# Retention and expert routing on one core: the last tiles' indirect transfers and the q, k, v loads tied to TensorE

## The chip, the cores and the metric

The kernel runs on one core of a Trainium2 chip. The engines of that core are TensorE (PE; its weight loads are listed as PEld), VectorE (DVE), ScalarE (ACT), GpSimd (POOL) and SyncE (SP), and 16 DMA engines move data. The metric is device microseconds of one execution; the comparison is of medians of several runs.

## The reference

Two parts follow each other. The first is an attention without softmax and with a decay per head; its output is cut into rows x of 512 numbers, one for each of the 4608 tokens. The second sends every token to the one expert of eight that has the largest logit.

```
ret = (q @ k.T / 8) * where(i >= j, gamma[h] ** (i - j), 0)       # 8 x 8 heads, 576 positions, 64 wide
x = (ret @ v) as rows [4608, 512]
logits = x @ w_gate;  e = argmax(logits);  p = softmax(logits)[e]
eom = sigmoid(x @ w_output_gate)[e]
out[token] = p * eom * (relu(x[token] @ w1[e]) @ w2[e])            # w1 512 x 1024, w2 1024 x 512
```

## The kernel before

The first phase goes through 36 tiles of 128 tokens (`for g in range(NTILE)`; nine tiles are two batches). The order on each engine is the order in which the code is written (`manual_schedule`). For a tile g TensorE computes the scores (`scores`, one tile ahead), the state's part and the tile's own part of the output (`out_x`), the update of the state (`update`) and the transposed k rows of the next tile (`k_rows`). GpSimd scales q (`prep_q`) and v (`prep_v`) by the decay, two tiles ahead and from tile 7 on three. ScalarE copies the output from PSUM (`xT`), VectorE turns it into rows (`x_rows`), and SyncE stores these to memory (`store_x`, tensor `xs`). The tensor `pack` holds q, k and v of a tile side by side; `load` fetches all of it, 768 KB, in one transfer into one of seven buffers `pk`, six tiles ahead from tile 8 on.

Every four tiles make a gate group: logits on TensorE, `gate_a` on VectorE (it begins with a transposition of the logits and ends with the choice `oh` and its count `cum`), `ranks` on TensorE, `gate_b`, `gate_d`, `gate_c`. The group then has four scatters, one for each tile, in the list `todo`: each writes a token's number, weight and row into `lst`, the list of its expert (`scatter`, an indirect DMA that GpSimd issues). Once the list's first rows are complete, `load_idx` reads them and `gather` fetches tokens' rows from `xs` by further indirect DMAs of GpSimd, into tiles `w2h`, `w2l` and later `x_q`. How many scatters and gathers go out in a tile is a table, `puts` and `mine`; nothing else holds GpSimd back from issuing them:

```
puts = {16: 2, 17: 2, 18: 0, 19: 0, 24: 2, 25: 2, 27: 2, 28: 2, 30: 0, 31: 0, 35: 5}.get(g, 1)
mine = {23: 1, 24: 1, 25: 1, 26: 1, 28: 1, 29: 2, 30: 1, 31: 1, 32: 1, 33: 2}.get(g, 0)
```

Behind the tiles the second phase begins: `mm1` is a strip of 12 products of the first expert matrix, and its argument `at` names products at which one entry of `todo` is issued. The first strip stands between the last logits and the last `ranks`. From here on gathers are tied to TensorE one at a time: `tc.add_manual_dep(i.ins, last[0].name, SYNC, ...)` makes GpSimd wait until the product `last[0]` is done. SyncE's transfers are issued in the order of the code; each waits until the eighth before it has landed.

Of the kernel before, what the change touches and what calls it, by code (L numbers as in the profile page):

```python
# [10 lines left out]
F32 = mybir.dt.float32  # L11
# [10 lines left out]
B, H, S, D = 8, 8, 576, 64  # L22
# [4 lines left out]
P = 128  # L27
NP = H // 2
# [23 lines left out]
def tile_retention_moe(  # L52
# [126 lines left out]
        xps.append(a[:, 1].rearrange("p (k n) -> p k n", k=KB))  # L179
    pools = {"xt0": xta, "ht0": hpa}  # L180

    last = [None]

    def gather(e, t, u, paced=False):
        if u == 0 and e == 0 and t < TA:
            make_gidx(0, t, t + 1, G)
        if u == 0 and (e, t) not in XG:
            XG[e, t] = pools["xq"].tile([P, 4, P], F32, name="x_q")
        seen = xs if e or t >= TA else xs[0:4 * P * (READY[t] + 1) * GT]
        i = G.indirect_dma_start(out=XG[e, t][:, u, :], out_offset=None, in_=seen,  # L190
                                 in_offset=bass.IndirectOffsetOnAxis(ap=gidx[:, e, 4 * t + u:4 * t + u + 1], axis=0))
        if paced:
            tc.add_manual_dep(i.ins, last[0].name, SYNC, reason="one gather to a stretch of products")

    def size(e, part):
        return N1[e] if part else R0[e]
# [171 lines left out]
    pk, qs, vs, kn, xT, xr, gt = {}, {}, {}, {}, {}, {}, {}  # L368
    st_ps, stcur = [None], [None]

    def load(g):
        pk[g] = ld.tile([P, 3, 512], F32, name="pk")
        SP.dma_start(out=pk[g], in_=pack[g])

    def load_first():
        for g in range(5):
            pk[g] = ld.tile([P, 3, 512], F32, name="pk")
        A.dma_start(out=pk[0][:, 0], in_=pack[0, :, 0])
        SP.dma_start(out=gq_sb[:, :, 0:P], in_=gq)
        SP.dma_start(out=pk[0][:, 1], in_=pack[0, :, 1])  # L380
        A.dma_start(out=cmat_sb[:, 0], in_=cmat[:, 0])
        SP.dma_start(out=ident, in_=ident_d)
        A.dma_start(out=pk[0][:, 2], in_=pack[0, :, 2])
        SP.dma_start(out=gkf, in_=gk)
        SP.dma_start(out=pk[1], in_=pack[1])
        SP.dma_start(out=wg_sb, in_=wg)
        SP.dma_start(out=pk[2], in_=pack[2])
        SP.dma_start(out=pk[3], in_=pack[3])
        SP.dma_start(out=pk[4], in_=pack[4])

    def more_gq(c):
        w = P if c < 4 else 64
# [6 lines left out]
    def prep_q(g):  # L399
        c = g % CPB  # L400
        c0 = P * c if c < 5 else 64 + P * (c - 5)
        qs[g] = pk[g][:, 0].rearrange("p (n i) -> p n i", n=NP)
        (V if g < 2 else G).tensor_tensor(out=qs[g], in0=qs[g], in1=gq_sb[:, :, c0:c0 + P], op=ALU.mult)

    def prep_v(g):
        v = vs[g] = pk[g][:, 2].rearrange("p (h d) -> p h d", d=D)
        n = 5 if g > 22 else 0
        for h in range(n):
            A.activation(out=v[:, h], in_=v[:, h], func=AF.Copy, scale=gk_sb[:, g % CPB, h])
        G.tensor_tensor(out=v[:, n:H], in0=v[:, n:H], in1=gk_sb[:, g % CPB, n:H].broadcast_to([P, H - n, D]),  # L410
                        op=ALU.mult)

    def k_rows(g):

        kt = ps_1.tile([P, 512], F32, name="kt")
        for p in range(NP):
            T.transpose(kt[:, P * p:P * p + P], pk[g][:, 1, P * p:P * p + P], ident)
        kn[g] = wk.tile([P, 512], F32, name="kn")
        if g % CPB == 4:
            for i in range(2):  # L420
                v = [a.rearrange("t (a b c) -> t a b c", a=2, b=2)[:, :, i] for a in (kn[g], kt)]
                A.activation(out=v[0], in_=v[1], func=AF.Copy, scale=half[:, i:i + 1])
        else:
            A.copy(out=kn[g], in_=kt)

    def scores(g):


        sc = [banks[(2 * g + r) % 3] for r in range(2)]
        S_sb = wk.tile([P, 2, NP, P], F32, name="S_sb")  # L430
        edge = g % CPB == 4
        for pp in (0, 2):
            for late in range(2):
                for p in (pp, pp + 1):
                    h = (late + p) % 2
                    i = slice(64, P) if late else slice(0, 64) if edge else slice(0, P)
                    for r in range(2):
                        s = slice(64 * r, 64 * r + 64)
                        T.matmul(sc[r][64 * h:64 * h + 64, p, i], lhsT=pk[g][s, 1, P * p + 64 * h:P * p + 64 * h + 64],  # L439
                                 rhs=qs[g][s, p, i], start=True, stop=True, skip_group_check=True)  # L440
        m = cmat_sb[:, 1 if edge else 0].rearrange("p (a b) i -> p a b i", a=1).broadcast_to([P, 2, 2, P])
        for r in range(2):
            V.tensor_tensor(out=S_sb[:, r].rearrange("p (a b) i -> p a b i", a=2),  # L443
                            in0=sc[r].rearrange("p (a b) i -> p a b i", a=2), in1=m, op=ALU.mult)
        return S_sb

    def update(g):
        c = g % CPB
        if c == 8:
            return  # L450
        if c in (0, 4):
            st_ps[0] = ps_1.tile([P, NP, D], F32, name="st_ps")
        for p in range(NP):
            for r in range(2):
                o = P * p + 64 * r
                T.matmul(st_ps[0][64 * r:64 * r + 64, p, :], lhsT=kn[g][:, o:o + D], rhs=vs[g][:, 2 * p + r, :],
                         start=(c in (0, 4) and p == 0), stop=True, skip_group_check=True)
        A.copy(out=stT[g % 2], in_=st_ps[0])
        stcur[0] = stT[g % 2]

    def out_x(g, S_sb, state):
        c = g % CPB
        o = o_ps[:, :, 256 * (g % 2):256 * (g % 2) + 256]
        part = lambda p, r: o[64 * ((p + r) % 2):64 * ((p + r) % 2) + 64, r, P * (p // 2):P * (p // 2) + P]
        order = [(p, (p + i) % 2) for p in range(NP) for i in range(2)]
        if state is not None:
            w = 64 if c == 4 else P
            for p, r in order:
                s = slice(64 * r, 64 * r + 64)
                T.matmul(part(p, r)[:, 0:w], lhsT=state[s, p, :], rhs=qs[g][s, p, 0:w],  # L470
                         start=(p < 2), stop=False, skip_group_check=True)
        for p, r in order:
            T.matmul(part(p, r), lhsT=vs[g][:, 2 * p + r, :], rhs=S_sb[:, r, p, :],
                     start=(state is None and p < 2), stop=True, skip_group_check=True)
# [589 lines left out]
```

## Time and profile before

| | |
|---|---|
| median of three runs | 588.22 us (586.67 to 591.13) |
| the profiled execution's own time | 594.7 us |
| its span in the profile | 592.6 us |
| mean granted TensorE clock | 0.98 |
| PE busy | 558.9 us, 94% |
| PEld busy | 519.0 us, 88% |
| DVE, ACT, POOL busy | 367.0, 179.0, 329.7 us |
| DMA | 105.86 MB, mean 179 GB/s |

The profile is of one execution, which took longer than the median of the runs. The first phase reaches to about 165 us of the span. A granted clock of 1.00 is 2.4 GHz and 0.50 is 1.2 GHz. An idle time is written in square brackets with what ended it; "issue" means that the profile shows nothing that the engine waited for, "remote" that the releasing event is not one of an instruction of the trace.

### The profile page before, as it was taken

The page shows a single profiled execution, that of the slowest core. Times are in us where ns is not written, and L with a number is a line of the kernel's source. Part 1 is how long each engine was busy: PE and PEld are TensorE (multiplying, and loading weights), DVE is VectorE, ACT ScalarE, POOL GpSimd, SP SyncE. Part 2 cuts the span into 40 slices and gives each one's busy share as a digit, 9 for nine tenths or more (in the row PEclk, how much of TensorE's full clock was granted, in tenths as well). Part 3 has the DMA queues.
Part 4 walks back from the last instruction along what each step waited for, and adds up shares of the span by engine and source line. Part 5 has one row for each costly group of instructions (what it writes and reads, how often), then busy time and mean ns, then how long its engine had stood idle before and what let it go on. Part 6 is the DMA issues. An engine that isn't in the chain of part 4 may idle for free. (4 is left out here: it accounts for less than half of the span.)

```text
span 592.6 us, 14974 instructions
## 1 busy us (share of the span) xinstructions
PE 558.9 (94%) x5886; PEld 519.0 (88%) x5886; DVE 367.0 (62%) x805; ACT 179.0 (30%) x419; POOL 329.7 (56%) x359
## 2 busy tenths in 40 slices
PE   6989998999769989999999999999999999999994
PEld 4878887778569989998999899899999989999993
DVE  3668887678547465884576378457636747755440
ACT  4524435566114122420421232042123204213011
POOL 3848886889454576664555264345527526624602
PEclk9989998999879999999999999999999999999999
DMA  8989987796102475645643664464356455543123
GB/s 335 363 294 324 299 294 251 232 322 205 59 25 70 132 206 177 207 147 146 193 151 106 189 202 132 112 221 158 113 178 213 141 145 167 166 124 130 45 56 114
DMA packets 50069, 105.86 MB, mean 179 GB/s; under 512 B 10190, under 2 KB 24719, under 8 KB 49998
## 3 DMA queue, kind: packets, MB, share of 16 engines
q1 hardware_dynamic: 40254, 84.53, 44.8%
q0 software_dynamic: 9312, 19.71, 10.3%
q8 instruction: 47, 0.77, 0.5%
q10 hardware_dynamic: 432, 0.66, 0.4%
q14 instruction: 24, 0.20, 0.1%
HBM read 79.67 MB, written 25.33 MB: 177 GB/s over the span
## 5 line engine op out<-in xcount | busy, mean ns | idle before, releaser
L190 POOL DMA_INDIRECT x_q<-xs,gidx x139 | 149.4, 1075 | 90.2 <-PE y_ps L289 36.5
L242 PE MATMUL h_ps<-xh,w1h 128*128 128x256 f32 (+5 forms) x512 | 154.1, 301 | 0.4 <-DVE hl L245 0.4
L242 PE MATMUL h_ps<-xl,w1h 128*128 128x256 f32 (+5 forms) x512 | 153.9, 301 | 0.3 <-DVE xl L224 0.3
L242 PE MATMUL h_ps<-xh,w1l 128*128 128x256 f32 (+5 forms) x512 | 153.7, 300 | 0.0
L242 PEld LDWEIGHTS h_ps<-xh,w1h 128*128 128x128 f32 x512 | 97.2, 190 | 1.3 <-DVE hl L245 0.7
L242 PEld LDWEIGHTS h_ps<-xl,w1h 128*128 128x128 f32 x512 | 97.1, 190 | 0.8 <-DVE xl L224 0.5
L242 PEld LDWEIGHTS h_ps<-xh,w1l 128*128 128x128 f32 x512 | 97.9, 191 | 0.0
L244 ACT ACTIVATE hh<-h_ps 128x256 fp32r<-128x256 f32 (+5 forms) x128 | 52.4, 415 | 134.9 <-PE h_ps L242 110.0
L245 DVE SCALAR_TENSOR_TENSOR hl<-h_ps,hh 128x256 fp32r<-128x256 f32 (+5 forms) x128 | 57.8, 458 | 51.9 <-ACT hh L244 41.5
L289 PE MATMUL y_ps<-hh,w2l 128*128 128x360 f32 (+3 forms) x256 | 81.2, 317 | 0.0
L289 PE MATMUL y_ps<-hl,w2h 128*128 128x360 f32 (+3 forms) x256 | 81.2, 317 | 0.0
L289 PE MATMUL y_ps<-hh,w2h 128*128 128x360 f32 (+3 forms) x256 | 81.2, 317 | 0.0
L443 DVE TENSOR_TENSOR S_sb<-sc,cmat_sb 128x512 f32<-128x512 f32 x72 | 45.9, 679 | 22.7 <-PE sc L439 21.0
L223 ACT CAST xh<-x_t 128x512 fp32r<-128x512 f32 (+4 forms) x36 | 21.3, 592 | 122.3 <-DVE x_t L219 84.8
L224 DVE TENSOR_TENSOR xl<-x_t,xh 128x512 fp32r<-128x512 f32 (+4 forms) x36 | 23.8, 660 | 53.5 <-ACT xh L223 51.1
L248 POOL DMA_INDIRECT out_dram<-y,idx x15 | 15.3, 1018 | 67.1 <-ACT y L272 60.4
L248 POOL DMA_INDIRECT out_dram<-yr,idx x24 | 26.7, 1113 | 44.1 <-ACT yr L315 42.5
L439 PE MATMUL sc<-pk 64*64 64x64 f32 (+1 forms) x1152 | 38.4, 256 | 12.6 <-issue 7.2
L439 PEld LDWEIGHTS sc<-pk 64*64 64x64 f32 x1152 | 30.6, 139 | 21.5 <-issue 20.0
L167 DVE TENSOR_TENSOR w1l<-st,w1h 128x1024 fp32r<-128x1024 f32 (+1 forms) x36 | 47.9, 1330 | 2.1
L263 PE MATMUL y_ps<-w2h,hl 128*128 128x512 f32 x120 | 46.8, 390 | 2.0 <-DVE hl L245 2.0
L575 POOL DMA_INDIRECT lst<-ents,sli x36 | 37.0, 1029 | 20.6 <-DVE ents L571 15.0
(137 smaller groups left out, 970.1 us busy)
## 6 DMA issues: line engine op xcount, KB each, us to landing
st<-in_w_dram SPq DMA_DIRECT2D x64, 512.0 KB
pk<-in_pack_dram SPq DMA_DIRECT2D x35, 768.0 KB
xs<-xq SPq DMA_DIRECT2D x36, 256.0 KB
yr<-yg SPq DMA_DIRECT2D x16, 256.0 KB
yg<-yt SPq DMA_DIRECT2D x16, 176.0 KB
x_q<-xs,gidx POOLq DMA_INDIRECT x139
yg<-yt SPq DMA_DIRECT2D x12, 160.0 KB
yr<-yg SPq DMA_DIRECT2D x4, 208.0 KB
```

What stands on the lines that cost most here:

```text
L167: V.tensor_tensor(out=lo[:, k], in0=st[:, k], in1=hi[:, k].bitcast(F32), op=ALU.subtract)
L190: i = G.indirect_dma_start(out=XG[e, t][:, u, :], out_offset=None, in_=seen, in_offset=bass.IndirectOffsetOnAxis(ap=gidx[:, e, 4 * t + u:4 ...
L224: return lambda: V.tensor_tensor(out=lo, in0=src[:, :, 0:n], in1=hi.bitcast(F32), op=ALU.subtract)
L242: last[0] = T.matmul(ps, lhsT=a[:, k, :], rhs=b[:, k, :], start=(j == 0), stop=(j == 3 * KB - 1)).ins
L244: A.activation(out=hh, in_=ps, func=AF.Relu)
L245: V.scalar_tensor_tensor(out=hl, in0=ps, scalar=0.0, in1=hh.bitcast(F32), op0=ALU.max, op1=ALU.subtract)
L248: i = G.indirect_dma_start(out=out, out_offset=bass.IndirectOffsetOnAxis(ap=rows, axis=0), in_=y, in_offset=None, bounds_check=NT - 1, oob ...
L263: last[0] = T.matmul(ps, lhsT=a[:, c0:c0 + n], rhs=b, start=(j == 0), stop=(j == 3 * FB - 1)).ins
L289: last[0] = T.matmul(ps[:, 0:n], lhsT=a, rhs=b, start=(j == 0), stop=(j == 3 * FB - 1)).ins
L439: T.matmul(sc[r][64 * h:64 * h + 64, p, i], lhsT=pk[g][s, 1, P * p + 64 * h:P * p + 64 * h + 64], rhs=qs[g][s, p, i], start=True, stop=Tru ...
L443: V.tensor_tensor(out=S_sb[:, r].rearrange("p (a b) i -> p a b i", a=2), in0=sc[r].rearrange("p (a b) i -> p a b i", a=2), in1=m, op=ALU.mult)
L575: i = G.indirect_dma_start(out=lst, out_offset=bass.IndirectOffsetOnAxis(ap=sli[:, t, :], axis=0), in_=ent[:, t], in_offset=None)
```

## The change

Two things change. First, the scatters and gathers of the last three tiles are tied to products of TensorE, two to a tile: the two gathers of tile 33 to the last state product (mark `q`) and the last own product (mark `v`) of that tile, two scatters each of tiles 34 and 35 likewise, and two more to the first strip's products. One scatter moves forward to tile 31. The load of the list for the fourth tile of the first expert moves behind the first strip. Second, `pack` is laid out with q, k and v one behind the other, and each is loaded by a transfer of its own into a buffer of its own; from the sixth tile on they wait for the marks `q`, `v` and `u` (the last product of `update`) of the tile six before.

```diff
+    last, marks = [None], {}
+    def gather(e, t, u, paced=False, by=None):
...
-        if paced:
-            tc.add_manual_dep(i.ins, last[0].name, SYNC, reason="one gather to a stretch of products")
+        if paced or by:
+            tc.add_manual_dep(i.ins, (by or last[0]).name, SYNC, reason="one gather to a stretch of products")
...
-    def load(g):
-        pk[g] = ld.tile([P, 3, 512], F32, name="pk")
-        SP.dma_start(out=pk[g], in_=pack[g])
+    def load(g, i, by=None):
+        pk[g, i] = ld.tile([P, 512], F32, name="qkv"[i])
+        j = SP.dma_start(out=pk[g, i], in_=pack[g, i])
+        if by:
+            tc.add_manual_dep(j.ins, by.name, SYNC, reason="one transfer to a stretch of products")
...
     def update(g):
         c = g % CPB
+        marks["u"] = marks["v"]
...
+                i = T.matmul(st_ps[0][64 * r:64 * r + 64, p, :], lhsT=kn[g][:, o:o + D], rhs=vs[g][:, 2 * p + r, :],
+                             start=(c in (0, 4) and p == 0), stop=True, skip_group_check=True)
+                marks["u"] = i.ins
...
+                marks["q"] = T.matmul(part(p, r)[:, 0:w], lhsT=state[s, p, :], rhs=qs[g][s, p, 0:w],
+                                      start=(p < 2), stop=False, skip_group_check=True).ins
+        marks.setdefault("q", last[0])
...
+            marks["v"] = T.matmul(part(p, r), lhsT=vs[g][:, 2 * p + r, :], rhs=S_sb[:, r, p, :],
+                                  start=(state is None and p < 2), stop=True, skip_group_check=True).ins
...
-        def scatter(t):
+        def scatter(t, by=None):
...
+            if by:
+                tc.add_manual_dep(i.ins, (by[0] if by is last else by).name, SYNC,
+                                  reason="one scatter to a stretch of products")
...
-        for t in (g + 5,) if g < 8 else (g + 5, g + 6) if g == 8 else (g + 6,):
-            if t < NTILE:
-                load(t)
+        if g == 0:
+            for i in range(3):
+                load(5, i)
...
-        puts = {16: 2, 17: 2, 18: 0, 19: 0, 24: 2, 25: 2, 27: 2, 28: 2, 30: 0, 31: 0, 35: 5}.get(g, 1)
-        mine = {23: 1, 24: 1, 25: 1, 26: 1, 28: 1, 29: 2, 30: 1, 31: 1, 32: 1, 33: 2}.get(g, 0)
+        puts = {16: 2, 17: 2, 18: 0, 19: 0, 24: 2, 25: 2, 27: 2, 28: 2, 30: 0, 33: 0, 34: 0, 35: 0}.get(g, 1)
+        mine = {23: 1, 24: 1, 25: 1, 26: 1, 28: 1, 29: 2, 30: 1, 31: 1, 32: 1}.get(g, 0)
...
+        if g == 33:
+            gather(0, *divmod(got, 4), by=marks["q"])
+            gather(0, *divmod(got + 1, 4), by=marks["v"])
+        elif g > 33:
+            for m in "qv":
+                todo.pop(0)(by=marks[m])
         x_rows(g)
...
         update(g)
+        if g + 6 < NTILE:
+            for i, m in enumerate("qvu"):
+                load(g + 6, i, marks[m])
...
-    load_idx(0, TA, TA + 1)
     gate_a(NG - 1)
     exp_a(NG - 1)
-    mm1(0, 0, 0)
+    todo[:] = [partial(f, by=last) for f in todo]
+    mm1(0, 0, 0, (1, 7))
+    load_idx(0, TA, TA + 1)
...
-        "pack": np.ascontiguousarray(np.stack([tr(nat(q)), tr(swapped(nat(k))), swapped(nat(v))], axis=2)),
+        "pack": np.ascontiguousarray(np.stack([tr(nat(q)), tr(swapped(nat(k))), swapped(nat(v))], axis=1)),
```

The up-front loads of tiles 0 to 4 are split in the same way. What moves on GpSimd is shown from the scatter of tile 32 on; `L575` is the scatter, `L190` a gather, `L559` a small addition for the next gate, and in brackets stand the semaphores waited for (DMASW: earlier indirect transfers; PE, DVE, Pool: engines). Before:

```order
L574 MEMSET tick 128x1
L575 DMA lst<-ents,sli 37888x16 [waits DMASW2_49,DVE_49]
L190 DMA w2l_107<-xs,gidx 128x128 [waits DMASW3_49]
L190 DMA w2l_107<-xs,gidx 128x128 [waits DMASW4_49]
L574 MEMSET tick 128x1 [waits Pool_49]
L575 DMA lst<-ents,sli 37888x16 [waits DMASW5_49]
L574 MEMSET tick 128x1 [waits Pool_49]
L575 DMA lst<-ents,sli 37888x16 [waits DMASW6_49]
L559 TENSOR_TENSOR base_81<-csm_sb,bump 128x1 [waits DVE_49]
L574 MEMSET tick 128x1 [waits Pool_49]
L575 DMA lst<-ents,sli 37888x16 [waits DMASW7_49]
L574 MEMSET tick 128x1 [waits Pool_49]
```

On GpSimd from the same scatter of tile 32 on, now (the scatter is `L580`, the addition `L564`):

```order
L579 MEMSET tick 128x1 [waits Pool_49]
L580 DMA lst<-ents,sli 37888x16 [waits DMASW3_49]
L190 DMA w2l_107<-xs,gidx 128x128 [waits DMASW4_49,PE_49]
L190 DMA w2l_107<-xs,gidx 128x128 [waits DMASW5_49,PE_49]
L579 MEMSET tick 128x1 [waits Pool_49]
L580 DMA lst<-ents,sli 37888x16 [waits DMASW6_49,PE_49]
L579 MEMSET tick 128x1 [waits Pool_49]
L580 DMA lst<-ents,sli 37888x16 [waits DMASW7_49,PE_49]
L564 TENSOR_TENSOR base_81<-csm_sb,bump 128x1 [waits DVE_49]
L579 MEMSET tick 128x1 [waits Pool_49]
L580 DMA lst<-ents,sli 37888x16 [waits DMASW0_49,DVE_49,PE_49]
L579 MEMSET tick 128x1 [waits Pool_49]
```

The instructions and their order are the same; two gathers and every scatter from here to the first strip wait for TensorE as well. On SyncE, around the weights' load (`L149`) of tile 10, `L373` is a load of q, k and v and `L485` the store of a tile's rows (DMAHW: earlier transfers of SyncE). Before:

```order
L373 DMA pk<-in_pack_dram 128x1536 [waits DMAHW7_49,PE_49,Pool_49]
L485 DMA xs<-xq 128x512 [waits DMAHW0_49,DVE_49]
L149 DMA st<-in_w_dram 128x1024 [waits DMAHW1_49]
L373 DMA pk<-in_pack_dram 128x1536 [waits DMAHW2_49,PE_49,Pool_49]
L485 DMA xs<-xq 128x512 [waits DMAHW3_49,DVE_49]
L373 DMA pk<-in_pack_dram 128x1536 [waits DMAHW4_49,PE_49,Pool_49]
```

On SyncE at the same place now (the store is `L490`):

```order
L490 DMA xs<-xq 128x512 [waits DMAHW5_49,DVE_49]
L149 DMA st<-in_w_dram 128x1024 [waits DMAHW6_49]
L373 DMA q<-in_pack_dram 128x512 [waits DMAHW7_49,PE_49]
L373 DMA k<-in_pack_dram 128x512 [waits DMAHW0_49,PE_49]
L373 DMA v<-in_pack_dram 128x512 [waits DMAHW1_49,PE_49,Pool_49]
L490 DMA xs<-xq 128x512 [waits DMAHW2_49,DVE_49]
L373 DMA q<-in_pack_dram 128x512 [waits DMAHW3_49,PE_49,Pool_49]
L373 DMA k<-in_pack_dram 128x512 [waits DMAHW4_49,PE_49]
```

One load of a tile has become three in a row, behind the store of the tile before instead of ahead of it, each with a wait for TensorE.

## Rows read from the trace of the kernel before

**Rows 1.** Stretches of 20 us: engines' busy us (instructions), TensorE's clock, DMA share, GB/s.
```profile
20.00:40.00 20.00, 17.51 (x405) 15.39 (x402) 13.25 (x30) 8.09 (x17) 16.71 (x16) 0.92 0.92 321
60.00:80.00 20.00, 19.12 (x484) 16.11 (x482) 17.32 (x36) 7.23 (x17) 16.43 (x21) 1.00 0.89 299
80.00:100.00 20.00, 17.52 (x417) 14.77 (x417) 15.94 (x42) 11.81 (x34) 17.99 (x23) 0.96 0.78 266
100.00:120.00 20.00, 18.52 (x383) 15.47 (x381) 12.57 (x32) 10.22 (x33) 14.45 (x21) 0.87 0.77 235
...
140.00:160.00 20.00, 16.54 (x331) 13.52 (x328) 12.10 (x33) 8.35 (x25) 13.33 (x18) 0.91 0.47 154
160.00:180.00 20.00, 14.78 (x137) 13.54 (x134) 10.51 (x41) 4.70 (x11) 10.32 (x19) 0.83 0.10 32
180.00:200.00 20.00, 20.00 (x124) 20.00 (x123) 13.37 (x46) 5.17 (x8) 9.59 (x10) 1.00 0.44 119
```

**Rows 2.** Timeline of TensorE and ScalarE, 147 to 157 us: start, us, what.
```profile
147.11 0.90 PE L439 MATMUL sc<-pk 64*64 64x128 f32 x32
147.83 0.69 PE L470 MATMUL o_ps<-pk,stT 64*64 64x128 f32 x16
...
149.68 0.71 PE L456 MATMUL st_ps<-pk,kn 128*64 128x64 f32 x16
...
150.90 0.79 PE L439 MATMUL sc<-pk 64*64 64x128 f32 x12
...
156.59 0.37 ACT L458 COPY stT<-st_ps 128x256 f32<-128x256 f32 x1 [4.61 <-remote]
...
156.97 0.21 PE L529 MATMUL lg_ps<-oh,cbf_sb 128*128 128x32 bf16 x1
```

**Rows 3.** Timeline of GpSimd, 149 to 169 us, four of ten indirect transfers.
```profile
149.22 1.03 POOL L575 DMA_INDIRECT lst<-ents,sli  x1 [0.17 <-issue]
150.56 0.97 POOL L190 DMA_INDIRECT w2l<-xs,gidx  x1 [0.30 <-issue]
...
154.40 0.98 POOL L575 DMA_INDIRECT lst<-ents,sli  x1 [0.19 <-issue]
...
167.61 0.97 POOL L575 DMA_INDIRECT lst<-ents,sli  x1 [0.19 <-issue]
```

**Rows 4.** Timeline of TensorE and VectorE from the last logits to the ranks.
```profile
164.02 1.06 PE L491 MATMUL lg_ps<-xT,wg_sb 128*32 128x128 f32 x26 [0.88 <-issue]
...
169.38 0.33 DVE L497 STREAM_TRANSPOSE lg_ps<-lg_ps 128x128 f32<-128x128 f32 x1 [4.20 <-remote]
...
171.13 0.18 PE L529 MATMUL lg_ps<-oh,cbf_sb 128*128 128x32 bf16 x1 [3.81 <-DVE oh L513]
```

**Rows 5.** Timelines of GpSimd and TensorE beside a pair of scatters.
```profile
119.12 0.96 POOL L575 DMA_INDIRECT lst<-ents,sli  x1 [0.18 <-issue]
...
119.92 0.45 PE L470 MATMUL o_ps<-pk,stT 64*64 64x128 f32 x5 [0.39 <-issue]
120.67 0.32 PE L470 MATMUL o_ps<-pk,stT 64*64 64x128 f32 x1 [0.30 <-issue]
```

**Rows 6.** Timeline of TensorE, its two longest "issue" stalls ahead of 140 us.
```profile
36.38 0.54 PE L470 MATMUL o_ps<-pk,stT 64*64 64x128 f32 x9 [1.29 <-issue]
...
98.92 0.68 PE L439 MATMUL sc<-pk 64*64 64x128 f32 x9 [2.36 <-issue]
```

**Rows 7.** DMA issues by the page: queue, count, size.
```profile
pk<-in_pack_dram SPq DMA_DIRECT2D x35, 768.0 KB
xs<-xq SPq DMA_DIRECT2D x36, 256.0 KB
```

**Rows 8.** A stretch of half a microsecond within the second stall, columns as in rows 1.
```profile
97.50:98.00 0.50, 0.00 (x0) 0.00 (x0) 0.50 (x2) 0.50 (x3) 0.50 (x1) 1.00 0.01 1
```

**Rows 9.** Timelines of SyncE and GpSimd: the load of tile 9, and the wait for it.
```profile
23.31 0.59 SPq L373 DMA_DIRECT2D pk<-in_pack_dram  x1
...
31.58 1.28 POOL L403 TENSOR_TENSOR pk<-pk,gq_sb 128x512 f32<-128x512 f32 x1 [0.73 <-DMA pk<-in_pack_dram]
```

More of the change, by code (lines that the diff above doesn't have):

```diff
@@ L180, in tile_retention_moe @@
     pools = {"xt0": xta, "ht0": hpa}
-    last = [None]
-    def gather(e, t, u, paced=False):
+    last, marks = [None], {}
+    def gather(e, t, u, paced=False, by=None):
         if u == 0 and e == 0 and t < TA:
@@ L369, in tile_retention_moe @@
     st_ps, stcur = [None], [None]
-    def load(g):
-        pk[g] = ld.tile([P, 3, 512], F32, name="pk")
-        SP.dma_start(out=pk[g], in_=pack[g])
+    def load(g, i, by=None):
[3 more added lines that the diff above has]
+            tc.add_manual_dep(j.ins, by.name, SYNC, reason="one transfer to a stretch of products")
     def load_first():
-        for g in range(5):
-            pk[g] = ld.tile([P, 3, 512], F32, name="pk")
-        A.dma_start(out=pk[0][:, 0], in_=pack[0, :, 0])
+        for i in range(3):
+            pk[0, i] = ld.tile([P, 512], F32, name="qkv"[i])
+        A.dma_start(out=pk[0, 0], in_=pack[0, 0])
         SP.dma_start(out=gq_sb[:, :, 0:P], in_=gq)
-        SP.dma_start(out=pk[0][:, 1], in_=pack[0, :, 1])
+        SP.dma_start(out=pk[0, 1], in_=pack[0, 1])
         A.dma_start(out=cmat_sb[:, 0], in_=cmat[:, 0])
         SP.dma_start(out=ident, in_=ident_d)
-        A.dma_start(out=pk[0][:, 2], in_=pack[0, :, 2])
+        A.dma_start(out=pk[0, 2], in_=pack[0, 2])
         SP.dma_start(out=gkf, in_=gk)
[L385 to L389, printed above, removed]
+        for g in range(1, 5):
+            for i in (0, 1, 2):
+                load(g, i)
+            if g == 1:
+                SP.dma_start(out=wg_sb, in_=wg)
     def more_gq(c):
@@ L401, in prep_q @@
         c0 = P * c if c < 5 else 64 + P * (c - 5)
-        qs[g] = pk[g][:, 0].rearrange("p (n i) -> p n i", n=NP)
+        qs[g] = pk[g, 0].rearrange("p (n i) -> p n i", n=NP)
         (V if g < 2 else G).tensor_tensor(out=qs[g], in0=qs[g], in1=gq_sb[:, :, c0:c0 + P], op=ALU.mult)
     def prep_v(g):
-        v = vs[g] = pk[g][:, 2].rearrange("p (h d) -> p h d", d=D)
+        v = vs[g] = pk[g, 2].rearrange("p (h d) -> p h d", d=D)
         n = 5 if g > 22 else 0
@@ L416, in k_rows @@
         for p in range(NP):
-            T.transpose(kt[:, P * p:P * p + P], pk[g][:, 1, P * p:P * p + P], ident)
+            T.transpose(kt[:, P * p:P * p + P], pk[g, 1][:, P * p:P * p + P], ident)
         kn[g] = wk.tile([P, 512], F32, name="kn")
@@ L438, in scores @@
                         s = slice(64 * r, 64 * r + 64)
-                        T.matmul(sc[r][64 * h:64 * h + 64, p, i], lhsT=pk[g][s, 1, P * p + 64 * h:P * p + 64 * h + 64],
+                        T.matmul(sc[r][64 * h:64 * h + 64, p, i], lhsT=pk[g, 1][s, P * p + 64 * h:P * p + 64 * h + 64],
                                  rhs=qs[g][s, p, i], start=True, stop=True, skip_group_check=True)
@@ L455, in update @@
                 o = P * p + 64 * r
-                T.matmul(st_ps[0][64 * r:64 * r + 64, p, :], lhsT=kn[g][:, o:o + D], rhs=vs[g][:, 2 * p + r, :],
-                         start=(c in (0, 4) and p == 0), stop=True, skip_group_check=True)
+                i = T.matmul(st_ps[0][64 * r:64 * r + 64, p, :], lhsT=kn[g][:, o:o + D], rhs=vs[g][:, 2 * p + r, :],
+                             start=(c in (0, 4) and p == 0), stop=True, skip_group_check=True)
+                marks["u"] = i.ins
         A.copy(out=stT[g % 2], in_=st_ps[0])
@@ L469, in out_x @@
                 s = slice(64 * r, 64 * r + 64)
-                T.matmul(part(p, r)[:, 0:w], lhsT=state[s, p, :], rhs=qs[g][s, p, 0:w],
-                         start=(p < 2), stop=False, skip_group_check=True)
+                marks["q"] = T.matmul(part(p, r)[:, 0:w], lhsT=state[s, p, :], rhs=qs[g][s, p, 0:w],
+                                      start=(p < 2), stop=False, skip_group_check=True).ins
+        marks.setdefault("q", last[0])
         for p, r in order:
-            T.matmul(part(p, r), lhsT=vs[g][:, 2 * p + r, :], rhs=S_sb[:, r, p, :],
-                     start=(state is None and p < 2), stop=True, skip_group_check=True)
+            marks["v"] = T.matmul(part(p, r), lhsT=vs[g][:, 2 * p + r, :], rhs=S_sb[:, r, p, :],
+                                  start=(state is None and p < 2), stop=True, skip_group_check=True).ins
         xT[g] = wk.tile([P, KB, P], F32, name="xT", bufs=6)
@@ L636, in tile_retention_moe @@
         n, late = divmod(g - GT, GT)
-        for t in (g + 5,) if g < 8 else (g + 5, g + 6) if g == 8 else (g + 6,):
-            if t < NTILE:
-                load(t)
+        if g == 0:
+            for i in range(3):
+                load(5, i)
         if g > 0:
```

## The prediction

> **What bounds the kernel now.** I read the table of 20 us stretches first. From 180 us on TensorE is busy for 20.00 of 20 us at full clock, in nearly all stretches as in the one shown, so whatever is saved before that point reaches the end of the run almost whole [rows 1]. The change works in the first 180 us, and there the worst stretches are 140 to 180 us: TensorE is busy 16.54 and 14.78 us of 20 and its granted clock averages 0.91 and 0.83 [rows 1]. Those are the last tiles of the first phase and the start of the expert products. The reader should see in [rows 2] a normal tile first: scores start at 147.11, the state products 0.72 us later, and the next tile's scores at 150.90, so a tile is 3.8 us. Then, from 150.90, the 32 score products of tile 35 that should need 0.72 us need until 156.97, in pieces with gaps that no semaphore of the profile explains.
>
> What runs beside it is GpSimd: five indirect transfers of about 1.0 us each with 0.3 us between them, from 149.22 to 155.38 [rows 3]. TensorE comes back about 1 us after the last. ScalarE's copy of the state starts at 156.59 after 4.61 us of waiting for a "remote" release, though the state products it reads ended at 150.4 [rows 2]. The same picture comes again with the next five, the last of which ends at 168.58 [rows 3]: the gate's transposition on VectorE starts at 169.38 after 4.20 us of "remote", 0.8 us after that scatter, though the logits ended at 165.1, and TensorE waits 3.81 us for it [rows 4]. So a row of indirect transfers without a pause holds up TensorE, and also what it has to tell the others. Why it does so no row shows; that the two go together, twice, is what I build on.
>
> **Indirect transfers.** The change issues the same number of them; it ties two gathers to tile 33, two scatters each to tiles 34 and 35, and two to the first strip of expert products. GpSimd gets no instruction more. The stalls that I charge to the two rows of five:
> - scores of tile 35: 156.97 - 150.90 - 0.72 = 5.35 us [rows 2];
> - the wait for the gate: 3.81 us. From VectorE's transposition to the ranks it takes 1.75 us (169.38 to 171.13), and the first strip's twelve products, 2 us, lie beside that; without the "remote" part this wait is nothing [rows 4];
> - half clock behind both: 20 x (1 - 0.91) = 1.8 us and 20 x (1 - 0.83) = 3.4 us [rows 1]; TensorE stood idle in part of it, so I count four fifths, 4.2 us.
>
> Together 13.4 us. The 0.88 us before the last logits are left out: there TensorE waits for ScalarE's copy of the last tile. What stays is the price of four pairs. The nearest row is a pair that ends with the scatter at 119.12: TensorE's gaps beside it are 0.39 + 0.30 = 0.69 us, and behind it nothing happens to the chain [rows 5]. But that pair had 1.3 us of other GpSimd work behind it, and these follow each other closer. The upper bound is the price in the rows of five, (5.35 + 3.81) / 10 = 0.92 us a transfer, 1.83 us a pair. I take 1.3 a pair, the middle: the transfers are as dense as in the rows of five, but a tied one can't start while TensorE is held up before its mark, so that the hold-up pauses its own cause. 4 x 1.3 = 5.2, so **8.2 us saved**; the ends are 13.4 - 2.8 = 10.6, and 13.4 - 7.3 - 4.2 = 1.9 if the half clock stays too. The added waits stand in front of nothing on GpSimd but later scatters and one small addition, whose reader comes a gate later.
>
> The list load that moves behind the first strip now waits for the two scatters tied to that strip as well, about 2 us. Its reader stands three strips later, some 6 us at full clock, which hides it; without that cover it costs those 2 us, inside my range.
>
> **Loads.** 35 transfers of 768 KB become three of 256 KB each [rows 7]; SyncE issues 70 more at 0.59 us or less each [rows 9], 41 us at most on a queue that stands idle for most of 150 us: nothing. A tile's store now stands behind three waits on TensorE, but each of these ends before VectorE has made the rows that the store reads. From tile 14 on a load goes out up to a tile later than before. Its v then has two tiles, 7.6 us, until GpSimd scales it, and TensorE needs it only three tiles after that; in the fullest stretch, tile 9's load of 768 KB issued at 23.31 was waited for until 31.58, 8.3 us [rows 9]. Where that comes back, GpSimd waits 0.7 us a tile, which its own idle time (16.43 us busy of 20, five tiles) covers [rows 1]. What could be gained are two long stalls in this stretch, 1.29 us at 36.38 and 2.36 us at 98.92 [rows 6], and the half clock of 0.92, 0.96 and 0.87 around them, 5.0 us by the same reckoning and 4.0 at four fifths [rows 1]: 7.7 us. If a big load in the way had caused them, spreading the loads would remove them. But in the second one the DMA engines were empty, 0.01 of their time and 1 GB/s [rows 8]: no load was passing. So I take 1 us of the 7.7, near to nothing, and keep 0 and 7.7 as ends; a loss is the slow rival below. The Trainium skill (Runtime: NRT & Kernel Launch, section Instruction fetch mechanics) says that engines stream their program in blocks and that crossing from one to the next is mostly hidden; whether a late block caused these stalls no row here shows. By that rule the loads would gain nothing, and the sum would be 8.2 us.
>
> **Sum.** 8.2 + 1.0 = 9.2 us of the profiled execution's 594.7, 1.55%. That execution lies 6.5 us above the median of the runs, so some of its stalls may be rarer in those; I scale by share: 588.22 x 0.9845 = 579.1, so **579 us**. The forecast's own range is 575 (nearly 10.6 + 1 saved, and a little of the loads) to 584, where the first rival begins.
>
> **The rivals.**
> 1. *The ties come too late to bind.* GpSimd is behind TensorE here: the first gather of tile 33 ran at 150.56 [rows 3], when that tile's state products had ended at 148.5 and the update behind its own products had begun at 149.68 [rows 2], and one scatter more now precedes it. A mark that has passed holds nothing back, so the transfers would run in a row as before; at 1.3 us each GpSimd needs 10.4 us for eight, about what TensorE needs for the stretch. Then the change doesn't do what it says, and only the low end of 1.9 us is saved: 586 us. Against it: once TensorE is held up, the next mark is not reached.
> 2. *The loads caused the long stalls.* Then 8.2 + 7.7 us go, 2.7%: 572 us. The empty DMA engines in [rows 8] speak against it.
> 3. *The thirds cost the DMA engines more (slower).* From 20 to 80 us these are 0.89 to 0.92 busy [rows 1], and loads are three quarters of a tile's bytes, 768 KB beside a store of 256 KB [rows 7]. If loads in thirds take half as much engine time again, 0.91 becomes 0.91 x (1 + 0.75 x 0.5) = 1.25: GpSimd and then TensorE wait for q, k and v, and 80 us become 100. Less the 9 saved that is 599 us. It decides from about 30% more, where 9 us are lost. Against it: whatever the mixture of sizes, the stretches move 305 (235 / 0.77) to 349 (321 / 0.92) GB/s for each full share of engine time [rows 1]; 14% lie between the worst and the best, and 14% on the loads makes 1.01, no loss yet. The Trainium skill (DMA: Bandwidth & Descriptors, section Rules for kernel authors) advises at least 1 MiB per DMA for bandwidth, which speaks against the change, and its fit of 2.0 us + bytes / 436e3 (made for GpSimd's path) gives, as an estimate, 2.6 us for a third and 3.8 us for the whole: paid one behind the other, 7.8 us a tile. With transfers overlapping at 0.92 busy the trace does not bear that out, so this has a small chance.
>
> **How the numbers follow.** Chances: forecast 0.54 (575 to 584), ties too late 0.20 (584 to 588), loads too 0.13 (568 to 575), costly thirds 0.10 (593 to 605), something else 0.03. Leaving out the costly thirds and the lower part of rival 2 gives the range **571 to 589**. The runs before spread by 0.8%, so 1%, below 582.3 or above 594.1, is about what can be told from no change. Faster by that: nine tenths of the forecast, and rival 2, 0.61; slower: most of the costly thirds and of the rest, 0.11; the remainder 0.28.
>
> **What would show it.** In the trace after: no stall of more than about 1.5 us on TensorE between the scores of tile 34 and the second strip; the gate's transposition within 1 us of the logits; no half clock behind 150 us; the pairs on GpSimd more than 2 us apart. If the gathers and scatters again stand in one row of five or more beside a halting TensorE, rival 1 holds. If the stalls near 36 and 98 us are gone without others in their place, rival 2. If GpSimd's scaling waits for q or v in tile after tile and the DMA engines are full, rival 3. I would be wrong altogether if the stutter came from something that only falls at the same time, TensorE's program itself for one: then it stays where it is, whatever GpSimd does.

## The result and the profile after

The changed kernel takes 583.48 us, median of 11 runs (581.47 to 585.51); the kernel before, run beside it, 588.55 us (11 runs, 585.98 to 592.11). The ratio is 0.9899 with a 95% interval of 0.9870 to 0.9928: 1.0% faster. Ratios, here and below, leave out executions that took over 1.5% longer than the fastest of their kernel; the medians keep them. The profiled execution after took 582.43 us with a span of 580.6 us.

The first view after is the table of stretches that answers to [rows 1] (busy us and instructions of PE, PEld, DVE, ACT and POOL, granted clock, DMA share, GB/s), with the 60 us in which the loads are densest, and one stretch cut to the half clock. Its first line is the kernel before's, for the same 60 us.

```profile
20.00:80.00 60.00, 56.42 (x1374) 48.46 (x1372) 45.78 (x107) 23.87 (x52) 46.62 (x53) 0.97 0.91 310
...
20.00:80.00 60.00, 55.89 (x1359) 47.37 (x1354) 46.37 (x108) 23.75 (x52) 45.92 (x53) 1.00 0.92 313
...
80.00:100.00 20.00, 19.33 (x470) 16.39 (x472) 17.27 (x47) 13.10 (x37) 17.20 (x22) 1.00 0.79 267
100.00:120.00 20.00, 18.25 (x414) 14.85 (x404) 13.00 (x40) 11.88 (x41) 17.79 (x26) 1.00 0.87 296
140.00:160.00 20.00, 16.82 (x278) 12.81 (x273) 11.63 (x33) 5.33 (x13) 12.75 (x21) 0.74 0.35 118
160.00:180.00 20.00, 20.00 (x128) 19.86 (x128) 16.91 (x61) 8.07 (x14) 11.82 (x16) 1.00 0.17 51
...
149.60:159.80 10.20, 8.14 (x93) 6.24 (x92) 5.58 (x18) 2.08 (x5) 4.48 (x9) 0.50 0.16 55
```

From 160 to 180 us TensorE is full, where before it still had 5.2 us of idle time and a clock of 0.83. But from 149.6 to 159.8 us the clock is at its lower level: the half clock did not go, it moved.

The next view is the timeline of TensorE and VectorE in the last two tiles and the first strip (start, us, what, idle before), which answers to [rows 2, 4].

```profile
145.60 0.90 PE L441 MATMUL sc<-q,k 64*64 64x128 f32 x32
...
147.91 0.42 PE L474 MATMUL o_ps<-q,stT 64*64 64x128 f32 x3 [0.30 <-issue]
148.65 0.27 PE L474 MATMUL o_ps<-q,stT 64*64 64x128 f32 x1 [0.31 <-issue]
...
150.11 1.35 PE L478 MATMUL o_ps<-S_sb,v 128*64 128x128 f32 x10 [0.43 <-issue]
...
154.05 1.13 PE L474 MATMUL o_ps<-q,stT 64*64 64x128 f32 x16 [1.53 <-ACT stT L462]
...
159.72 0.33 DVE L502 STREAM_TRANSPOSE lg_ps<-lg_ps 128x128 f32<-128x128 f32 x1 [0.79 <-PE lg_ps L496]
...
161.79 0.19 PE L534 MATMUL lg_ps<-oh,cbf_sb 128*128 128x32 bf16 x1
...
161.95 0.41 PE L242 MATMUL h_ps<-xh,w1h 128*128 128x360 f32 x1
```

The scores of tile 35 (145.60) come in one piece. A little of the stutter is left in the state products behind them: 0.30, 0.31 and 0.43 us, then 1.53 us. The gate's transposition starts as soon as the logits end, and the ranks follow the first strip without a wait; the 4.20 us of "remote" and the 3.81 us behind it [rows 4] are gone.

On GpSimd, beside [rows 3]:

```profile
147.12 0.96 POOL L190 DMA_INDIRECT w2l<-xs,gidx  x1 [0.30 <-issue]
148.39 0.94 POOL L190 DMA_INDIRECT w2l<-xs,gidx  x1 [0.30 <-issue]
...
150.70 0.99 POOL L580 DMA_INDIRECT lst<-ents,sli  x1 [1.25 <-remote]
...
151.99 0.97 POOL L580 DMA_INDIRECT lst<-ents,sli  x1 [0.19 <-issue]
...
155.50 0.99 POOL L580 DMA_INDIRECT lst<-ents,sli  x1 [2.00 <-PE o_ps L474]
...
157.38 0.98 POOL L580 DMA_INDIRECT lst<-ents,sli  x1 [0.78 <-PE o_ps L478]
...
160.42 0.97 POOL L580 DMA_INDIRECT lst<-ents,sli  x1 [1.95 <-PE h_ps L242]
```

The two gathers of tile 33 follow the scatter ahead of them with the usual 0.30 us: their marks had passed. From tile 34 on four of the six tied scatters wait, for 1.25, 2.00, 0.78 and 1.95 us, though the first of these waits is put down to "remote" and not to TensorE. What was a row of five and five is now a row of three and three pairs.

**Where the profiled execution's 12.3 us come from** (594.7 less 582.43), by three points that both timelines have. The scores of tile 35 start at 145.60 instead of 150.90: 5.3 us, all from ahead of the last tiles. From there to the second strip it takes 16.35 us (161.95) instead of 20.5 (171.4, where the last ranks stand before): 4.2 us. From the second strip to the end of the span it is 418.65 instead of 421.2 us: 2.5 us, for the half clock that before lay behind the gate wait, to 176.9 us. The last 0.3 us lie outside the span.

### The profile page after: what moved, and what is told of

The parts are those of the page before. It is cut to its first block, busy times and chain, and to the rows that moved or that the text cites. A ratio compares the mean times of both kernels' runs of the same rounds, so it can differ in the third digit from the quotient of the medians.

```text
span 580.6 us, 15140 instructions
## 1 busy us (share of the span) xinstructions
PE 554.3 (95%) x5886; PEld 513.6 (88%) x5886; DVE 366.2 (63%) x805; ACT 179.0 (31%) x419; POOL 330.6 (57%) x359
## 5 line engine op out<-in xcount | busy, mean ns | idle before, releaser
L190 POOL DMA_INDIRECT x_q<-xs,gidx x139 | 150.3, 1081 | 85.1 <-PE y_ps L289 32.7
L580 POOL DMA_INDIRECT lst<-ents,sli x36 | 37.5, 1042 | 21.0 <-DMA xs<-xq 5.9
L289 PEld LDWEIGHTS y_ps<-hh,w2h 128*128 128x128 f32 x256 | 48.1, 188 | 0.5 <-issue 0.5
L289 PEld LDWEIGHTS y_ps<-hl,w2h 128*128 128x128 f32 x256 | 48.1, 188 | 0.0
L289 PEld LDWEIGHTS y_ps<-hh,w2l 128*128 128x128 f32 x256 | 48.1, 188 | 0.0
```

Of the source, the lines that this page charges most:

```text
L289: last[0] = T.matmul(ps[:, 0:n], lhsT=a, rhs=b, start=(j == 0), stop=(j == 3 * FB - 1)).ins
```

## The experiments

Two theories stood at the start. That of the prediction: a row of indirect transfers on GpSimd without a pause holds TensorE up, so the ties bring the gain. Its rival: the gain comes from somewhere else, from the loads or from TensorE's own program at this place. The runs were made on three chips, called 1, 2 and 3 here; on each the kernel before was run beside them, and ratios are to that. One execution of e1_ties_only (1080.36 us) and the profiled one of e6_none_in_tiles (1079.88) took nearly twice as long as the others; the trace of the second is not used. The table has the time from the scores of tile 35 to the second strip in each trace, worked out from the timelines as above.

| kernel | chip | median us | ratio, 95% interval | tile 35 to second strip, us |
|---|---|---|---|---|
| before | 1 | 589.98 | 1 | 20.5 (first trace) |
| e1_ties_only | 1 | 583.91 | 0.9901, 0.9859 to 0.9943 | 14.6 |
| e2_loads_only | 1 | 586.41 | 0.9948, 0.9916 to 0.9980 | 19.4 |
| e3_thirds_untied | 1 | 587.49 | 0.9971, 0.9937 to 1.0005 | 18.2 |
| e4_whole_tied | 1 | 586.53 | 0.9951, 0.9918 to 0.9985 | 21.9 |
| before | 2 | 577.74 | 1 | no trace |
| a1_after_again | 2 | 576.22 | 0.9981, 0.9953 to 1.0009 | 13.0 |
| e5_row_at_13 | 2 | 576.08 | 0.9991, 0.9966 to 1.0017 | 13.6 |
| e6_none_in_tiles | 2 | 578.76 | 1.0015, 0.9986 to 1.0044 | no trace used |
| e7_none_whole | 2 | 580.67 | 1.0060, 1.0025 to 1.0094 | 11.8 |
| before | 3 | 578.39 | 1 | 13.6 (b0_before_again, 580.05, one run) |
| a2_after_again | 3 | 577.97 | 1.0006, 0.9966 to 1.0047 | 13.3 |
| e8_row_at_13_again | 3 | 575.16 | 0.9961, 0.9925 to 0.9997 | 13.5 |
| e9_none_in_tiles_again | 3 | 578.61 | 1.0011, 0.9977 to 1.0045 | 13.5 |

The first trace and the one after have no chip on record; the medians of their comparison are those of chip 1.

### Chip 1: the two parts apart

**e1_ties_only**: the kernel before with the ties, the new table and the first strip's two scatters; loads of 768 KB as before.

```diff
+        if g == 33:
+            gather(0, *divmod(got, 4), by=marks["q"])
+            gather(0, *divmod(got + 1, 4), by=marks["v"])
+        elif g > 33:
+            for m in "qv":
+                todo.pop(0)(by=marks[m])
```

> The kernel before with the tied scatters and gathers alone; loads are whole, as before. Theory A (the gain is that of the ties at the end of the first phase): 0.990 of the time before, as the whole change. Theory B (the gain is that of the loads): 1.000, within 0.2%. If both parts add: about 0.995. In the trace, by A, the 6 us scores of tile 35 and the 3.8 us wait for the gate are gone or halved.

Timeline of TensorE and GpSimd of this kernel:

```profile
146.93 0.46 PE L470 MATMUL o_ps<-pk,stT 64*64 64x128 f32 x4 [0.23 <-issue]
147.68 0.44 PE L470 MATMUL o_ps<-pk,stT 64*64 64x128 f32 x4 [0.29 <-issue]
148.38 0.43 PE L470 MATMUL o_ps<-pk,stT 64*64 64x128 f32 x2 [0.26 <-issue]
...
149.71 0.99 POOL L576 DMA_INDIRECT lst<-ents,sli  x1 [1.19 <-PE o_ps L470]
...
153.02 0.67 PE L470 MATMUL o_ps<-pk,stT 64*64 64x128 f32 x16 [2.55 <-ACT stT L458]
...
154.24 0.99 POOL L576 DMA_INDIRECT lst<-ents,sli  x1 [1.74 <-PE o_ps L470]
...
159.83 0.41 PE L242 MATMUL h_ps<-xh,w1h 128*128 128x360 f32 x1
```

The ratio is 0.9901, that of the whole change. The ties bind as in the changed kernel, the stutter lasts for the three transfers that still stand in a row (144.87, 146.20 and 147.47) and ends with the first pause of GpSimd, and the gate wait is gone. What stays beside the next pair (149.71 and 151.00) is the 2.55 us wait for ScalarE's copy of the state, which takes 0.53 us where nothing holds it up (146.62 us in a1, below). The ratio is what theory A named.

**e2_loads_only**: the changed kernel with the table and the first strip of before, no tie on an indirect transfer. **e3_thirds_untied**: as e2, and the thirds are issued where the kernel before issues its loads, without ties. **e4_whole_tied**: as e2, but one load of 768 KB for a tile, tied to the last state product. The edits in e3 and e4:

```diff
-            for i, m in enumerate("qvu"):
-                load(g + 6, i, marks[m])
+        for t in (g + 5,) if g < 8 else (g + 5, g + 6) if g == 8 else (g + 6,):
+            if t < NTILE:
+                for i in range(3):
+                    load(t, i)
...
-            for i, m in enumerate("qvu"):
-                load(g + 6, i, marks[m])
+            load(g + 6, marks["q"])
```

> The changed kernel with the table, the order of the list load and the first strip of the kernel before: only the loads are changed (thirds, tied). Theory A: 1.000, within 0.2%. Theory B: 0.990, and the long stalls near 36 and 98 us with their half clock are gone in the trace while the rows of five indirect transfers and the wait of 3.8 us stay. If both parts add: about 0.995.

> As the kernel with the loads alone, but the three transfers of a tile are issued where the kernel before issued its one, with no wait for products. If splitting is what helps (q is there before v): the same as the loads alone. If the ties are: 1.000. If thirds by themselves cost (the slow rival): above 1.003.

> The kernel before with whole loads of 768 KB, each issued behind the state products of the tile six before and tied to them, the rest as before. If the ties (the later, even issue) are what helps: the same as the loads alone. If only thirds help: 1.000 or a little more, since the load comes later as one piece.

Timeline of TensorE in e2, three of eight pieces of tile 35's scores and the gate wait:

```profile
148.99 0.45 PE L441 MATMUL sc<-q,k 64*64 64x128 f32 x3 [0.28 <-issue]
149.73 0.49 PE L441 MATMUL sc<-q,k 64*64 64x128 f32 x6 [0.29 <-issue]
...
151.93 0.42 PE L441 MATMUL sc<-q,k 64*64 64x128 f32 x2 [0.51 <-issue]
...
167.39 0.18 PE L534 MATMUL lg_ps<-oh,cbf_sb 128*128 128x32 bf16 x1 [2.96 <-DVE oh L518]
```

And of TensorE in e4:

```profile
152.97 1.13 PE L472 MATMUL o_ps<-pk,stT 64*64 64x128 f32 x16 [5.51 <-issue]
...
160.41 1.91 PE L494 MATMUL lg_ps<-xT,wg_sb 128*32 128x128 f32 x26 [3.83 <-ACT xT L479]
```

Without the ties the stutter is back. In e2 it stands as in [rows 2, 4], with a gate wait of 2.96 us. In e3 the scores are whole, the state and own products behind them come in pieces (147.36 to 151.03 us, gaps of 0.20 to 0.30), and the gate wait is 0.83 us. In e4 there is one halt of 5.51 us and one of 3.83 ahead of the last logits, beside ten transfers on GpSimd (144.97 to 158.50) with at most 0.73 us between them, and no gate wait. The same products stand at the same place of TensorE's program in e1 and after, where the transfers pause; so "TensorE's program itself" falls on this chip as the whole cause. Still each of e2 to e4 is some 0.3 to 0.5% faster than the kernel before, e3 with an interval that touches 1. Part of that may be the comparison, since the kernel before itself came out at 588.55 and at 589.98 us. No one edit is common to the three, and what they gain by is not settled. The gains do not add: 0.9901 by 0.9948 would be 0.985, and both parts together give 0.9899, in a comparison of their own.

### Chip 2: it does not stutter

**a1_after_again** is the changed kernel itself. **e5_row_at_13** puts a row elsewhere: the scatters of tiles 9 to 12 are held back and go out in tile 13.

```diff
-        puts = {16: 2,
+        puts = {9: 0, 10: 0, 11: 0, 12: 0, 13: 5, 16: 2,
```

**e6_none_in_tiles** takes the scatters out of tiles 34 and 35 and puts them into the first two strips, tied; **e7_none_whole** is the same with the 768 KB loads of before.

```diff
-        elif g > 33:
-            for m in "qv":
-                todo.pop(0)(by=marks[m])
...
-    mm1(0, 0, 0, (1, 7))
+    mm1(0, 0, 0, (1, 4, 7, 10))
...
+    todo[:] = [f if f.keywords else partial(f, by=last) for f in todo]
-    mm1(0, 0, 1)
+    mm1(0, 0, 1, (0, 2, 4, 6, 8, 10))
```

> The changed kernel again, beside the ones of this call: 0.990. If its stretch without half clock ahead of 140 us is its own and not chance, the profile shows none again; if it is chance, one or two may appear.

> The changed kernel, with the scatters of tiles 9 to 12 held back and given out at tile 13, four of them in a row, far from the end of the phase. Theory A: beside that row TensorE's products come in pieces with gaps of about 0.4 us, 2.5 to 4 us in all, and the time grows by 0.4 to 0.9% against the changed kernel. Rival (it is the program's place, not the row): no gap there, the same time within 0.2%.

> The changed kernel, but the scatters tied to tiles 34 and 35 go to the first two strips of expert products (four and six scatters there, all tied to products). Theory A (transfers without a pause hold TensorE up): the stutter of the last tiles shrinks to that of the two gathers, the half clock behind it goes, some 5 us more are saved: 0.982 of the time before. Rival (the stutter belongs to TensorE's own program at that place, or to the gathers): 0.990, with the stutter where it was. If the strips suffer from ten scatters instead of six, the strips' products come slower than 0.17 us apart.

> The same late scatters, but with the whole loads of the kernel before. If the loads of the change are worth something beside the ties: 0.3 to 0.5% slower than the late scatters with tied thirds. If they aren't: the same within 0.2%.

Here the kernel before takes 577.74 us, 2% less than on chip 1, and the change makes no difference that can be told (0.9981, interval over 1). Ahead of 140 us a1's clock falls once (0.91 from 120 to 140 us), so that the trace after has no fall there was chance. Timelines of GpSimd and TensorE in a1:

```profile
146.41 0.97 POOL L190 DMA_INDIRECT w2l<-xs,gidx  x1 [0.30 <-PE st_ps L459]
146.62 0.67 PE L474 MATMUL o_ps<-q,stT 64*64 64x128 f32 x16 [0.53 <-ACT stT L462]
...
148.93 0.99 POOL L580 DMA_INDIRECT lst<-ents,sli  x1 [0.19 <-issue]
149.00 1.06 PE L496 MATMUL lg_ps<-xT,wg_sb 128*32 128x128 f32 x26 [0.34 <-ACT xT L481]
...
152.13 0.43 PE L242 MATMUL h_ps<-xh,w1h 128*128 128x360 f32 x1 [2.07 <-ACT xh L223]
```

GpSimd issues nine transfers from 145.07 to 156.44 with 0.3 us between them: TensorE runs ahead of it, every mark has passed, and no tie binds. That is the prediction's first rival. Yet TensorE does not stutter beside this row; it waits only for ScalarE. So a row alone is not enough, and e5 to e7 can't tell a row from a place here: nothing stutters at tile 13, and taking all scatters out of the last tiles gains nothing (e6), so neither number of its expectation applies. With whole loads that version (e7) is 0.3% slower than with thirds (580.67 against 578.76; the two intervals overlap) and 0.6% slower than the kernel before, clear of its interval.

### Chip 3: the kernel before without the stutter

What was missing was a trace of the kernel before on a chip of this sort. The changed kernel and two of those of chip 2 were run again beside it. In these expectations theory A is that of the prediction, and theory B that the stutter depends on the chip.

> The unchanged kernel once more, for its trace. The chip is the question: on one chip the row of transfers of tiles 34 and 35 went with pieces of 0.3 to 0.5 us of idle time between score products, on another it did not, though nine transfers stood in a row there. Theory A (a row of transfers always holds TensorE up): the scores of tile 35 take 5 us or more instead of 0.7, and the gate wait is 3 to 4 us. Theory B (it depends on the chip): where the total of this kernel is about 577 us the scores take less than 1.5 us and the gate wait is under 1.5 us; where it is about 588 us both stand as in the first trace.

> The changed kernel once more, beside the kernel before on the same chip. Theory A: ratio 0.990. Theory B: 0.990 where the kernel before stutters in tile 35 in the run beside it, and 0.997 to 1.000 where it does not.

> Scatters of tiles 9 to 12 held back and issued in a row in tile 13. Where the kernel before stutters in tile 35: theory A (the row holds TensorE up wherever it stands) has the scores of tile 13 in pieces with gaps of 0.3 us and more, 2.5 to 4 us in all; the rival (the place in the program: it happens only near the end of the first phase) has scores of 0.7 to 0.9 us there, as on the other chip (ratio to before as for the changed kernel, within 0.3%). Where the kernel before does not stutter both expect nothing.

> No scatter in tiles 34 and 35; they stand tied in the first two strips of expert products. Where the kernel before stutters: theory A has no stutter in tiles 34 and 35 and scatters beside strip products at little cost, 0.3% below the changed kernel; the rival (TensorE's own program) has the pieces of 0.3 us in tiles 34 and 35 all the same. Where it does not: 1.001 to 1.002, as before on the other chip.

**b0_before_again** is the unchanged kernel. Its GpSimd and TensorE in the last tiles:

```profile
145.74 0.90 PE L439 MATMUL sc<-pk 64*64 64x128 f32 x32
...
146.81 0.67 PE L470 MATMUL o_ps<-pk,stT 64*64 64x128 f32 x16
...
149.01 0.97 POOL L190 DMA_INDIRECT w2l<-xs,gidx  x1 [0.30 <-issue]
149.85 0.67 PE L470 MATMUL o_ps<-pk,stT 64*64 64x128 f32 x16 [0.52 <-ACT stT L458]
...
151.53 1.00 POOL L575 DMA_INDIRECT lst<-ents,sli  x1 [0.19 <-issue]
152.23 1.06 PE L491 MATMUL lg_ps<-xT,wg_sb 128*32 128x128 f32 x26 [0.30 <-ACT xT L476]
...
155.19 0.43 PE L242 MATMUL h_ps<-xh,w1h 128*128 128x360 f32 x1 [1.89 <-ACT xh L223]
...
159.35 0.44 PE L242 MATMUL h_ps<-xh,w1h 128*128 128x360 f32 x1
```

The same program, with ten transfers in a row (147.68 to 160.42), has tile 35's scores in one piece and no gate wait; from them to the second strip it needs 13.6 us, where the first trace needs 20.5. The changed kernel on this chip needs 13.3, and its ratio is 1.0006. All four runs fit theory B in their traces, and the first of them rules out A as it stood. The row at tile 13 (e8) leaves one gap there, at 62.86 us in TensorE's timeline with 0.68 us of "issue", and the scores of the next tile are whole. e5 has the like at 61.81 us, 0.58 us; both are of the kind that ends with a block of the program landing, shown below with the loads, and no row's price. e8's ratio of 0.9961 lies below 1 by its interval, which neither theory has and e5, the same edit, does not repeat (0.9991); beyond the intervals neither is better than the changed kernel, and no other version is either.

## Why the prediction came out as it did

**The bound, and where the gain lies: right.** The time went out of the last tiles and the first strip, and what was saved there reached the end, as [rows 1] promised.

**The two rows of transfers: the mechanism is right on the chip of the comparison, and its price is off in one term.** Of the 13.4 us charged to stutter, gate wait and half clock, the prediction let 4 pairs keep 1.3 us each, 5.2 us. The trace after has 0.30 + 0.31 + 0.43 + 1.53 = 2.6 us of stalls in their place, so pairs cost half of what was taken. (The 1.53 us contain 0.53 that also stood before, at 161.10 us, and that the prediction did not count.) The step that failed is the next one, "no half clock behind 150 us": all 4.2 us were counted as saved. But the small stalls that stayed are followed by 10.2 us at a granted clock of 0.50 with TensorE busy for 8.14 of them, which at full clock would take half, so 4.1 us are still paid. That is as much as before, when it lay in two stretches: 0.91 and 0.83 over 20 us each [rows 1] make 10.4 us at half. 13.4 - 2.6 - 4.1 = 6.7 us, 1.13% of 594.7, where 8.2 were forecast; measured are 1.01%. The two timelines give the same 6.7 us (4.2 and 2.5, above). How long the half clock lasts is not fixed by the ties, though: e1, with the same ties and 3.3 us of stalls, has 0.83 from 150 to 160 us, 3.4 us at half, and so has b0, which does not stutter at all.

**Its premise was too general.** "A row of indirect transfers without a pause holds up TensorE" is true in the six traces of chip 1 and of the comparison: the stutter is there in all four kernels whose row is not broken, and it is cut short in both in which ties break it. On chips 2 and 3 a row of nine or ten does nothing. e5 and e8, which were to show whether the place in the program has a part, fell on chips that don't stutter. But every kernel also issues three pairs of scatters 0.3 us apart far from the end of the phase, between 104 and 135 us. Here is one in the kernel before, the pair's second scatter and the products beside it:

```profile
113.62 0.96 POOL L575 DMA_INDIRECT lst<-ents,sli  x1 [0.19 <-issue]
...
114.37 0.35 PE L439 MATMUL sc<-pk 64*64 64x64 f32 x5 [0.33 <-issue]
115.10 0.28 PE L439 MATMUL sc<-pk 64*64 64x64 f32 x2 [0.38 <-issue]
```

And in a1 on chip 2, where the products pass it whole:

```profile
113.89 0.96 POOL L580 DMA_INDIRECT lst<-ents,sli  x1 [0.19 <-issue]
...
114.53 0.66 PE L419 MATMUL kt<-ident,k 128*128 128x128 f32 x4
```

In the six traces of chip 1 and of the comparison 15 of these 18 pairs have a gap of this kind beside them, 0.20 to 0.59 us; on chips 2 and 3 none of 21 has. In all six TensorE passes the lone scatters ahead of 100 us without such a gap. So the stutter goes with transfers close behind each other, at several places of the program, and not with one place. What differs between the chips no row here shows (the runs on each were made together, so "chip" stands for all that was the same within them), nor by which path the transfers reach TensorE. The prediction said that no row shows why the two go together, and then gave no chance to a row that does no harm; on chips 2 and 3 there was nothing to save.

**The first rival: real, in part.** On chip 1 the two gathers' ties come too late (147.12 and 148.39 us), the others bind. The argument against it, that a TensorE that is held up does not reach its next mark, is what the two sorts of chips show: where it stutters the ties bind, where it does not they don't.

**The loads: forecast 1.0 us, within the noise of the sum; where the long stalls come from the prediction left open, and the traces show it.** The profiled execution gained 5.3 us ahead of tile 35. But e1, with whole loads, has these scores at 145.19 us too, and no half clock ahead of 154 us. In the medians the ties alone give as much as the whole change, so the 7.7 us of the second rival are ruled out; alone the loads give 0.5%, where 0.2% was forecast.

The long stalls of [rows 6] stand at fixed products of TensorE's program, in kernel after kernel. The first is after seven of a tile's 16 state products. After the change, in e1 and in a1, with nine products left each time:

```profile
34.78 0.54 PE L474 MATMUL o_ps<-q,stT 64*64 64x128 f32 x9 [1.02 <-issue]
...
36.02 0.54 PE L470 MATMUL o_ps<-pk,stT 64*64 64x128 f32 x9 [0.47 <-issue]
...
34.89 0.54 PE L474 MATMUL o_ps<-q,stT 64*64 64x128 f32 x9 [0.27 <-issue]
```

The second, 2.36 us before, is 0.99 in e1 (95.58 us) and 2.85 in e7 (98.54 us), again with nine score products left. What ends them is in the list of DMA packets, where one queue carries instructions, 47 packets of 16 KB in every trace; here the line of the page before (queue, kind, packets, MB, share of 16 engines):

```profile
q8 instruction: 47, 0.77, 0.5%
```

By the times of these packets all 41 "issue" stalls of 0.15 us or more on chips 2 and 3, up to 180 us, and all 24 of the other six traces ahead of 100 us (e6 left out), end 0.96 to 1.46 us after one has landed (in the kernel before 97.62 us, then 98.92). That the queue is TensorE's is inferred from this. So these stalls fit late blocks of the program, the cause that the prediction named without a row. The stutter is not of this kind: in the kernel before no such packet is under way from 150.46 to 159.70 us. [rows 8] was a stretch of half a microsecond near the end of a stall and says little of why the packet came late; in the 2 us ahead of the packets the DMA engines were busy 1.03 (32.10 to 34.10 us) and 0.67 (94.70 to 96.70 us) of the time. Added up ahead of 140 us, the late blocks cost 3.5 to 9.2 us in the five traces with whole loads and 0.9 to 3.8 us in the eight with thirds. That may be what thirds gain, but each is one execution, e4 gains as much with whole loads, and the medians of a1 and a2 show no such gain over the kernel before, so it is not shown.

**The costly thirds: ruled out.** From 20 to 80 us the DMA engines moved 313 GB/s at 0.92 of their time with thirds, and 310 at 0.91 before; e2 and e3 are not slower than the kernel before. The Trainium skill (DMA: Bandwidth & Descriptors, section Rules for kernel authors) advises at least 1 MiB per DMA; between 768 and 256 KB, with transfers overlapping, these two rows do not show that price.

**What was to show it.** The gate's transposition 0.03 us behind the logits: right. Pairs more than 2 us apart: right, from start to start (148.39 to 150.70, 151.99 to 155.50, 157.38 to 160.42). No stall above about 1.5 us: at the edge, 1.53. No half clock behind 150 us: wrong. Rival 2's sign came in part: the stall near 36 us stays (1.02 us), that near 98 us shrinks to 0.44 (96.33 us). That the forecast was taken off the median and not off the profiled execution mattered as much as the terms: 594.7 to 582.43 is 2.1%, the medians 1.0%.

## What to carry to other kernels

A stall that repeats beside another engine's work in one trace is a cause to test and not yet a rule: see the same program on a second chip before a general price is put on it. Where indirect transfers do hold TensorE up, a few products between pairs of them shorten it (9.2 us lost before, 2.6 us of stalls after), and the ties cost nothing that can be told where they don't (0.9981 and 1.0006). Do not count a fall of the clock as saved because most of the stalls ahead of it go: the 2.6 us that stayed were followed by as much half clock as the 9.2. An "issue" stall that stands at the same product in every version points to the program's place; look whether an instruction packet has just landed before a neighbour is blamed.

## What the runs showed of the hardware

- The same program takes 590 us on one chip (33 runs) and 578 on two others (35 and 29). In the two traces of it, 594.7 and 580.05 us, 6.9 us of the difference stand between the scores of tile 35 and the second strip (20.5 against 13.6).
- The stutter has a step: in e2 the pieces of the scores start at 148.28, 148.99, 149.73 and 150.48 us, 0.71 to 0.75 us apart, each with a few products and a gap of 0.27 to 0.51 us, while transfers start every 1.3 us. No row read here has this period.
- Products of the strips run at 0.165 us each at full clock beside scatters (160.14 to 161.62 us after), and in e1 on chip 1 at 0.163 (158.19 to 159.17 us); e3 has one gap of 0.39 us there. So not all of TensorE's work is held up by a transfer.
- On all three chips TensorE has stalls of 0.16 to 2.85 us that end 0.96 to 1.46 us after a 16 KB instruction packet has landed, two of them at the same product in several versions of the kernel.
